# A new order table for attention with a causal conv gate: fewer masks on GpSimd, fewer unread products, and buffers named at another step

## The chip, the cores and the metric

The kernel runs on 1 core of one Trainium2 chip. The metric is the device time of one execution in microseconds (us), as a median of repeated runs. The engines are TensorE (PE; PEld is its weight load), VectorE (DVE), ScalarE (ACT), GpSimd (POOL) and SyncE (SP), which issues most of the transfers.

## What is computed

Eight batches, eight heads, 576 positions, head size 64. Each head is causal attention with a decay bias from cumulated gates s. The joined heads (512 wide) go through a causal convolution of five taps, a sigmoid, a product with a projection, and an output projection.

```python
def _attn_ref(q, k, v, s):                       # 8, 8, 576, 64
    scores = (1.0 / np.sqrt(D)) * np.matmul(q, k.transpose(0, 1, 3, 2))
    cum = np.cumsum(np.maximum(s, 0.0), axis=-1)
    bias = -(cum[:, :, :, None] - cum[:, :, None, :])
    scores = np.where(causal, -1000000000.0, scores + np.minimum(bias, 0.0))
    attn = softmax(scores)
    return np.matmul(attn, v)

def _moe_ref(x, w_val, conv_w, w_out):           # x: 8, 576, 512
    for k in range(5):
        gate_pre += conv_w[k][None, None, :] * xp[:, k:k + S, :]
    return (1.0 / (1.0 + np.exp(-gate_pre)) * (x @ w_val)) @ w_out
```

## The kernel before

The whole program is one straight line of named steps. A table, ORDER, lists them as `name.indices:engine:slots`. The engine letter is S (SP), T (PE), A (ACT), V (DVE) or G (POOL); the slots say which PSUM banks or which of several buffers the step writes. A loop at the end of `main_path` walks the table and calls the function of each step, so that each engine gets its instructions in the order of the table, and waits are set where one step needs another's data or buffer. There is no scheduler behind it.

The work falls into 32 units, numbered n: batch n // 4 and pair of heads n % 4. For each unit:

- `ld_q`, `ld_k`, `ld_t`, `ld_v` load q, k, their last 64 rows (the tails) and v. `c_q`, `c_k` cast to bf16. `qt`, `qq`, `tt` transpose on PE, and `qe`, `te` copy the result from PSUM into QKT. Batch 0 is loaded by pairs of heads, the other batches whole or in halves.
- `s0`, `s1`, `s2` are three groups of score products into two PSUM banks, `e0`, `e1`, `e2` the exponentials of 2 x 512 columns into a P buffer (L556). The causal triangle of the four diagonal blocks, which lie in group 0, is masked in one of two ways. Either POOL clears it after the exponential (`mk`, an affine_select on 128 x 1024, L579), or PE adds a large negative number before it by two more products into the same banks (`future`, L518). `s4`, `e4` do the last 64 keys.
- `vp` scales v by the decay (POOL, L474); `av0`, `av` are P times V, 60 products a unit (L594); `rec`, `nm` divide by the sums; `xt` transposes back, `xe` copies to xT.
- The five taps: `t1` on DVE starts gp; each of `t2`, `t3`, `t4` is either one DVE instruction (L670), or a product `p2`, `p3`, `p4` on POOL (L654) or ACT (L652) into a pr buffer and an add `t` on POOL (L673). All taps of a unit update the same gp buffer in the table's order.
- `th` is the tanh of the gate on ACT, `val` the projection (L703), `glu` the gate product on DVE (L712). `out` is the output projection (L723), `oe` copies it to an ot buffer (ACT or DVE), `st` stores it.

The last four units, 28 to 31, are cut into two parts (positions 0 to 383 and 384 to 575) with names of their own: `u0` to `u3` for scores, `f0` to `f3` for exponentials of 128 x 768 (L570), `ml` for the small mask. Their other steps carry the part as a second index.

`wu` is an unread product: 512 columns of the identity times the identity into a bank that nobody reads (L620). `chk0` and `chk` look whether all reciprocals and conv ratios are in a safe range (L734 to L746), `cnt`, `cntc` and `flag` reduce that to one number, and every engine reads it for the final branch (L754, L807); a general path behind it isn't taken here.

Of the kernel before, what the change touches and what calls it, by code (L numbers as in the profile page):

```python
# [16 lines left out]
B, H, S, D = 8, 8, 576, 64  # L17
# [180 lines left out]
centre:V s0.1:T:4+5:1 ld_k.1.0:S:2 s2.1:T:2+3 e0.1:A qt.0.2.q:T:1 c_k.0.2:V decT:T:0 ld_cw:S e2.0:A qt.0.2.k:T:4
mk.1:G wu.20:T:5 ld_k.1.1:S qe.0.2.k:V wu.21:T:5 wu.22:T:5 qe.0.2.q:A s1.1:T:6+7 c_k.0.3:V e2.1:A s0.2:T:4+5:2
c_q.0.3:G ld_v.0.2:S expw:A qt.0.3.q:T:1 e1.1:A s4.0.1:T:2+3 qe.0.3.q:V vp.0.0:G qt.0.3.k:T:0 qe.0.3.k:V e4.0.1:A  # L200
ld_q.1.0:S:3 e0.2:A s2.2:T:6+7 s1.2:T:2+3 vp.0.1:G av0.0:T:0+1 e2.2:A av.0:T ld_v.0.3:S mk.2:G rec.0:V av0.1:T:4+5
e1.2:A nm.0:V av.1:T c_k.1.0:G:2 s0.3:T:6+7:0 rec.1:V s2.3:T:2+3 e0.3:A nm.1:V ld_t.1:S cwT:T:0 xt.0:T:1 c_k.1.1:G
cwc:V xt.1:T:4 e2.3:A wu.23:T:6 xe.0:V ld_q.1.1:S vp.0.2:G qq.1.1:T:0:7 t1.0:V:0 s4.0.2:T:2+3 s1.3:T:5+6 e4.0.2:A
xe.1:V c_q.1.0:A:0 s4.0.3:T:2+3 mk.3:G t3.0:V ld_v.1.2:S e4.0.3:A t1.1:V:1 e1.3:A ld_v.1.1:S av0.2:T:2+3 vp.0.3:G
av.2:T t2.0:V ld_v.1.0:S qe.1.3:A tt.1:T:5 ld_v.1.3:S qe.1.2:V p4.1:G:0 p4.0:A:1 ld_v.1.4:S ld_wv:S:4 av0.3:T:6+7
av.3:T te.1:A rec.2:V ld_t.2:S t4.1:G c_q.1.1:G nm.2:V s0.6:T:0+1:1 rec.3:V xt.2:T:5 nm.3:V e0.6:A t4.0:G s0.7:T:2+3:2
xe.2:V s2.6:T:6+7 e0.7:A qq.1.0:T:0:1 t1.2:V:2 mk.6:G p2.1:A:0 s1.6:T:2+3 t3.2:V qe.1.0:A ld_q.2:S:0 mk.7:G qe.1.1:V
e2.6:A t3.1:V s1.4:T:0+1 e1.6:A s0.4:T:6+7:0 t2.2:V ld_k.2:S:1 xt.3:T:4 e0.4:A s0.5:T:2+3:0 t2.1:G t4.2:V s2.4:T:6+7
xe.3:V wu.24:T:5 e2.4:A vp.1.0:G mk.4:G wu.25:T:5 t1.3:V:3 wu.26:T:5 wu.27:T:5 ld_wo:S:2 wu.28:T:5 e1.4:A s4.1.3:T:6+7
ld_t.3:S t3.3:V wu.29:T:5 wu.30:T:5 e4.1.3:A s1.5:T:0+1 t4.3:V wu.31:T:5 th.2:A:0 ld_q.3:S:3 vp.1.2:G av0.4:T:6+7  # L210
th.1:A:1 av.4:T t2.3:V e0.5:A vp.1.1:G cast_wv:G rec.4:V av0.6:T:4+5 nm.4:V av.6:T e1.5:A s2.5:T:2+3 rec.6:V
s1.7:T:6+7 nm.6:V e2.5:A xt.4:T:0 ld_v.2.2:S c_q.2:G:1 tt.2:T:1 xe.4:V th.0:A:2 av0.5:T:2+3 t1.4:V:2 av.5:T te.2:A
ld_v.2.4:S val.3.0:T:4 th.3:A:3 p4.4:G:1 rec.5:V val.3.1:T:1 nm.5:V e1.7:A val.1.0:T:5 glu.3.0:V t4.4:G xt.5:T:2
c_k.2:A:2 glu.3.1:V ld_v.2.1:S val.1.1:T:3 glu.1.0:V s2.7:T:6+7 glu.1.1:V qq.2.0:T:1:5 vp.1.3:G xe.5:V val.0.0:T:3
t2.4:V e2.7:A val.0.1:T:4 t1.5:V:1 p2.5:G:0 qe.2.0:A av0.7:T:6+7 glu.0.0:V glu.0.1:V ld_v.2.3:S val.2.0:T:3 t2.5:G
p3.5:A:1 t3.4:V av.7:T ld_v.2.0:S qe.2.1:A qq.2.1:T:4:2 ld_k.5:S:4 rec.7:V cast_wo:G nm.7:V val.2.1:T:0 qe.2.3:A
xt.6:T:5 glu.2.0:V xt.7:T:1 xe.6:V qe.2.2:A s0.9:T:6+7:1 glu.2.1:V s1.9:T:2+3 p4.5:G:0 xe.7:V out.0.2:T:0 e0.9:A
t1.6:V:0 out.0.0:T:4 t3.5:G t1.7:V:3 e1.9:A ld_k.3:S:0 t4.6:V s1.8:T:6+7 oe.0.2:A:0 s0.8:T:2+3:0 mk.9:G oe.0.0:A:1
t3.7:V val.7.0:T:0 e0.8:A ld_t.4:S out.0.3:T:4 t2.6:V p3.6:G:1 e1.8:A t2.7:V out.0.1:T:2 t3.6:G th.4:A:4 t4.7:V
val.4.0:T:3 st.0.2:S val.7.1:T:7 glu.4.0:V th.7:A:3 val.4.1:T:1 t4.5:G oe.0.3:V:2 th.6:A:1 ld_v.3.2:S s2.8:T:5+6  # L220
glu.7.1:V s4.2.3:T:3+4 glu.7.0:V e2.8:A val.6.0:T:7 glu.4.1:V vp.2.0:G val.6.1:T:0 glu.6.0:V e4.2.3:A ld_v.3.3:S
oe.0.1:V:3 s0.10:T:5+6:2 th.5:A:2 c_q.3:G:0 s2.9:T:3+4 glu.6.1:V av0.8:T:1+2 e2.9:A av.8:T val.5.0:T:0 ld_q.5:S:1
e0.10:A rec.8:V nm.8:V vp.2.1:G s2.10:T:3+4 val.5.1:T:7 e2.10:A glu.5.0:V s1.10:T:1+2 glu.5.1:V s0.11:T:5+6:0 vp.2.2:G
# [616 lines left out]
```

## Time and profile before

| | us |
|---|---|
| three runs | 188.97, 189.09, 189.77; median 189.09 |
| profiled execution, first to last instruction | 187.6 |
| PE busy / DVE / ACT / POOL in it | 170.1 / 163.3 / 170.6 / 164.5 |
| first full exponential starts | 7.85 |
| last full exponential (unit 27) starts | 150.28 |
| last gate product starts | 181.77 |

The page gives no time of its own for the profiled execution beside its span; the median is 1.5 us above the span. The matmuls' ends are modelled, so PE's busy time is no measure of how full PE is. Transfers keep the 16 DMA engines near full until about 130 us and nearly idle afterwards, apart from the stores.

### The profile page before, as it was taken

Reading aid. Unit: us, or ns where it says so; the run is one execution under the profiler, and the core shown is the slowest. Engines: PE = TensorE matmul, PEld = TensorE weight load, DVE = VectorE, ACT = ScalarE, POOL = GpSimd, SP = SyncE. Lnnn points to the kernel's source line nnn. Section 1 sums busy time; section 2 is a strip of 40 time slices with the busy share of each in tenths; the row PEclk is TensorE's granted clock in tenths of the full one; section 3 lists DMA queues with packets and bytes.
Section 4 is the critical chain, followed back from the end, with each engine's and each line's share of the span. In section 5 each row is a group of like instructions: output and inputs, shape, how many; then the busy total and the mean of one; then the engine's idle time right before and its main releaser. Section 6 shows DMA issues by size and latency. Waiting matters only on the chain.

```text
span 187.6 us, 6637 instructions
## 1 busy us (share of the span) xinstructions
PE 170.1 (91%) x2704; PEld 113.5 (60%) x2720; DVE 163.3 (87%) x321; ACT 170.6 (91%) x230; POOL 164.5 (88%) x149
## 2 busy tenths in 40 slices
PE   6898885888899998998978999999999999999991
PEld 2556573476757765576745667586566865776560
DVE  4355999878997899999999899998989899999980
ACT  2589899899999999999999999999999999999772
POOL 5267999899999999999978999999999989899610
PEclk9999999999999999999999999999999999999999
DMA  5998999999999999999298999899541003401164
GB/s 164 274 277 246 231 225 243 343 388 341 193 232 304 277 303 258 389 270 283 71 248 184 274 333 325 193 314 247 164 162 66 3 0 115 171 3 56 61 224 175
DMA packets 62283, 40.46 MB, mean 216 GB/s; under 512 B 47333, under 2 KB 49381, under 8 KB 62250
## 3 DMA queue, kind: packets, MB, share of 16 engines
q1 hardware_dynamic: 61706, 39.49, 77.1%
q8 instruction: 22, 0.36, 0.8%
q10 hardware_dynamic: 544, 0.52, 0.8%
q14 instruction: 11, 0.09, 0.2%
HBM read 30.57 MB, written 9.44 MB: 213 GB/s over the span
## 4 chain that ended last, share of the span: by engine, by line
PE 50%; ACT 15%; SPq 9%; DMA 8%; issue 6%; POOL 5%; DVE 4%; ACTq 0%; POOLq 0%; DVEq 0%
PE bank L723 14%; PE bank L703 11%; PE bank L594 10%; ACT P L556 9%; PE bank L505 7%; DMA vst<-in_v_dram 6%; SPq L435 3%; PE bank L629 3%; PE bank L626 3%; POOL gp L673 2%; DMA first<-in_k_dram 2%; ACT th L690 2%; SPq L471 2%; ACT QKT L373 2%; SPq L467 2%
## 5 line engine op out<-in xcount | busy, mean ns | idle before, releaser
L556 ACT ACTIVATE P<-bank 128x1024 bf16<-128x1024 f32 x84 | 82.9, 1042 | 4.1 <-PE bank L505 3.0
L670 DVE SCALAR_TENSOR_TENSOR gp<-bank,cwr,gp 128x574 f32<-128x574 bf16 (+6 forms) x72 | 52.3, 740 | 0.9 <-POOL gp L673 0.5
L673 POOL TENSOR_TENSOR gp<-gp,pr 128x572 f32<-128x572 f32 (+6 forms) x36 | 45.1, 1259 | 4.4 <-DVE gp L670 1.7
L474 POOL TENSOR_TENSOR Vp<-vst,w 128x650 bf16<-128x650 f32 x32 | 40.7, 1288 | 2.8 <-DMA vst<-in_v_dram 1.8
L505 PE MATMUL bank<-QKT 64*128 64x128 bf16 (+4 forms) x592 | 37.2, 237 | 4.8 <-ACT P L556 1.8
L703 PE MATMUL bank<-xT,wv 128*128 128x288 bf16 (+2 forms) x256 | 38.5, 287 | 1.1 <-ACT P L556 0.5
L594 PE MATMUL bank<-Vp,P 128*128 128x65 bf16 x960 | 36.0, 194 | 2.4 <-POOL Vp L474 1.1
L594 PEld LDWEIGHTS <-P 128*128 128x128 bf16 x960 | 33.2, 97 | 6.8 <-issue 1.5
L723 PE MATMUL bank<-wo,glu 128*128 128x512 bf16 x128 | 34.1, 380 | 1.5 <-issue 0.5
L505 PEld LDWEIGHTS <-QKT 64*128 64x128 bf16 x592 | 19.4, 94 | 22.3 <-issue 14.6
L712 DVE SCALAR_TENSOR_TENSOR glu<-th,bank 128x288 bf16<-128x288 f32 (+2 forms) x64 | 27.5, 445 | 2.0 <-ACT th L690 0.9
L703 PEld LDWEIGHTS <-wv 128*128 128x128 bf16 x256 | 22.4, 97 | 11.0 <-issue 4.8
L654 POOL TENSOR_TENSOR pr<-xT,cwr 128x572 f32<-128x572 bf16 (+6 forms) x28 | 28.3, 1020 | 0.6 <-ACT xT L373 0.6
L373 ACT COPY QKT<-bank 128x1024 bf16<-128x1024 bf16 (+1 forms) x26 | 24.2, 966 | 3.8 <-PE bank L489 2.9
L613 DVE TENSOR_TENSOR xn<-bank,recs 128x640 bf16<-128x640 f32 (+2 forms) x36 | 26.8, 745 | 0.6
L665 DVE SCALAR_TENSOR_TENSOR gp<-xT,cwr,bank 128x576 f32<-128x576 bf16 (+2 forms) x36 | 26.4, 741 | 0.7
L579 POOL TENSOR_SCALAR_AFFINE_SELECT P<-P 128x1024 bf16<-128x1024 bf16 (+1 forms) x22 | 22.3, 1021 | 4.2 <-ACT P L556 4.2
L690 ACT ACTIVATE th<-gp,cwr 128x576 f32<-128x576 f32 x28 | 22.0, 794 | 0.1
L723 PEld LDWEIGHTS <-glu 128*128 128x128 bf16 x144 | 12.4, 98 | 13.2 <-issue 1.6
L373 ACT COPY ot<-bank 128x512 f32<-128x512 f32 x26 | 15.2, 610 | 1.5 <-PE bank L723 1.0
L626 PE MATMUL bank<-ident,xn 128*128 128x128 bf16 x164 | 14.9, 219 | 0.7 <-ACT P L556 0.3
L373 POOL CAST qkb<-qkf 128x2048 bf16<-128x2048 f32 (+1 forms) x9 | 14.4, 1619 | 0.0
(66 smaller groups left out, 174.8 us busy)
## 6 DMA issues: line engine op xcount, KB each, us to landing
out_dram<-ot SPq DMA_DIRECT2D x36, 256.0 KB, 4.3
vst<-in_v_dram SPq DMA_DIRECT2D x28, 256.0 KB, 5.9
first<-in_q_dram SPq DMA_DIRECT2D x6, 512.0 KB, 6.0
first<-in_k_dram SPq DMA_DIRECT2D x6, 512.0 KB, 6.2
qkf<-in_q_dram SPq DMA_DIRECT2D x6, 512.0 KB, 6.7
qkf<-in_k_dram SPq DMA_DIRECT2D x6, 512.0 KB, 7.3
vst<-in_v_dram SPq DMA_DIRECT2D x15, 128.0 KB, 5.4
first<-in_q_dram SPq DMA_DIRECT2D x4, 256.0 KB, 5.3
```

The costliest lines, as they stand in the source:

```text
L373: (act.copy if e is act else e.tensor_copy)(dst, src)
L474: e.tensor_tensor(Vps[b % 2][:, :, HP[p]], vslot(b)[:, :, HP[p]], w[:, :, b * 8 + 2 * p:b * 8 + 2 * p + 2].unsqueeze(3).to_broadcast([128, ...
L505: pe.matmul(ps[:, hh, c0:c0 + nq], QKTs[b % 2][r, 1, p, k0:k0 + 128], QKTs[b % 2][r, 0, p, q0:q0 + nq], **kw)
L556: act.activation(out=Pt(n)[:, :, step * 512:(step + 1) * 512], in_=pair((f"s{step}", n)), func=AF.Exp, scale=0.125)
L594: pe.matmul(ps[:, o:o + 65], lhsT, Vps[b % 2][:, kb, 2 * p + w, :], start=(kb == 0), stop=(kb == qb))
L613: vec.tensor_tensor(xns[b % 2][:, g, p * 128:(p + 1) * 128].rearrange("t g (w d) -> t w g d", w=2), ps[:, :, :, 0:64], recs[:, n, :, g].un ...
L654: pool.tensor_tensor(pr, xTs[b % 2][:, c, 4 + lo - m:4 + hi - m], r.to_broadcast([128, hi - lo]), ALU.mult)
L670: vec.scalar_tensor_tensor(gp[:, lo:hi], xps(n, *h)[:, lo - m:hi - m], r, gp[:, lo:hi], ALU.mult, ALU.add)
L673: pool.tensor_tensor(gp[:, lo:hi], gp[:, lo:hi], prs[at[f"p{m}", n, *h][0]][:, lo:hi], ALU.add)
L703: pe.matmul(ps, wv[:, dc, c * 128:(c + 1) * 128], xTs[b % 2][:, dc, 4 + lo:4 + hi], start=(dc == 0), stop=(dc == 3))
L712: vec.scalar_tensor_tensor(glu2[:, c, o + lo:o + hi], th[:, lo:hi], 1.0, ps, ALU.add, ALU.mult)
L723: pe.matmul(bank_of(u, i), glu2[:, c, i * 128:i * 128 + 128], wo[:, c, :], start=(c == 0), stop=(c == 3))
```

## The change

The table is replaced as a whole. Counted by kind:

| step | before | after |
|---|---|---|
| masks on POOL (`mk`, `ml`) | 18 and 4 | 4 and 0 (units 3, 11, 12, 22) |
| unread products | 32 | 12 |
| casts of q and k: ACT, DVE, POOL | 3, 4, 17 | 2, 2, 20 |
| tap products: ACT, POOL | 8, 28 | 4, 36 |
| tap adds `t2` to `t4`: DVE, POOL | 72, 36 | 68, 40 |
| QKT copies: ACT, DVE | 26, 10 | 23, 13 |
| output copies: ACT, DVE | 26, 10 | 28, 8 |
| xT copies: ACT, DVE | 12, 24 | 11, 25 |

The loads and stores keep their number. The units still come in nearly the same sequence; within a unit the score groups and exponentials may now come in any order, so the P buffer is named at the exponential (slot of `e0` to `e2`, `f0` to `f3`) and not at `s0`. The numbers of buffers (BUFS) are the same.

```diff
-ld_k.0.0:A ld_q.0.0:S ld_k.0.1:A wu.0:T:0 ld_t.0:S wu.1:T:7 wu.2:T:0 wu.3:T:7 ld_s:S wu.4:T:0 ld_q.0.1:S wu.5:T:7
+ld_k.0.1:A ld_t.0:S ld_k.0.0:A ld_q.0.0:S ld_q.0.1:S ld_k.0.2:S ld_k.0.3:S ld_s:S ld_v.0.0:S wu.0:T:7 wu.1:T:6
...
-    Pt = lambda n, h=None: Ps[at["s0" if h is None else f"u{2 * h}", n][1]]
+    split = lambda n: n in splits
+
+    def Pt(n, h=None):
+        steps = ("e0", "e1", "e2") if h is None else (f"f{2 * h}", f"f{2 * h + 1}")
+        return Ps[next(at[f, n] for f in steps if (f, n) in at)[0]]
...
-            split = ("u0", n) in at
-            g = ((3, 1)[h] if split else 4)
-            d = Pt(n, h if split else None)[:, :, 0:128 * g].rearrange("k w (g q) -> k w g q", g=g)
+            g = ((3, 1)[h] if split(n) else 4)
+            d = Pt(n, h if split(n) else None)[:, :, 0:128 * g].rearrange("k w (g q) -> k w g q", g=g)
...
-        two = at["val", n, 0][0]
-        j = two[hf] if isinstance(two, list) else at["val", n, hf][0]
+        j = at["val", n, hf][0]
...
+    splits = {int(name.split(".")[1]) for name, *_ in steps if name.startswith("u0.")}
```

The first place is SP, the start of the program. `first` is the tile that takes q and k of batch 0, `tail` the last 64 rows of all heads, `gp` holds s here, `vst` holds v. Before:

```order
L430 DMA first<-in_q_dram 128x2x256
L458 DMA tail_105<-in_q_dram 64x8x64
L458 DMA tail_105<-in_k_dram 64x8x64
L376 DMA gp_121<-in_s_dram 64x576
L430 DMA first<-in_q_dram 128x2x256 x2
L430 DMA first<-in_k_dram 128x2x256
L467 DMA vst_92<-in_v_dram 128x4x64 x2
L468 DMA vst_92<-in_v_dram 64x2x64
```

And after:

```order
L458 DMA tail_105<-in_q_dram 64x8x64
L458 DMA tail_105<-in_k_dram 64x8x64
L430 DMA first<-in_q_dram 128x2x256 x2
L430 DMA first<-in_k_dram 128x2x256 x2
L376 DMA gp_121<-in_s_dram 64x576
L467 DMA vst_92<-in_v_dram 128x4x64 x2
L468 DMA vst_92<-in_v_dram 64x2x64
```

The two tails moved ahead of the first q tile, and s moved behind four tiles of q and k. ACT's queue issues the first two k tiles in both.

The second place is POOL in the split units near the end. `gp` is the sum of taps, `pr` a tap product, `P` a buffer of exponentials; a pr row is a product, a gp row an add. Before:

```order
L673 TENSOR_TENSOR gp_119<-gp_119,pr_134 128x380
L579 AFFINE_SELECT P_118<-P_118 128x2x128
L654 TENSOR_TENSOR pr_134<-xT_114,cwr 128x381
L673 TENSOR_TENSOR gp_119<-gp_119,pr_135 128x382
L673 TENSOR_TENSOR gp_121<-gp_121,pr_134 128x381
L579 AFFINE_SELECT P_116<-P_116 128x2x128
L654 TENSOR_TENSOR pr_135<-xT_114,cwr 128x380
```

And after (L657 is the product and L676 the add in the new file):

```order
L657 TENSOR_TENSOR pr_135<-xT_114,cwr 128x381
L676 TENSOR_TENSOR gp_120<-gp_120,pr_135 128x381
L657 TENSOR_TENSOR pr_135<-xT_114,cwr 128x382
L676 TENSOR_TENSOR gp_120<-gp_120,pr_135 128x382
L676 TENSOR_TENSOR gp_122<-gp_122,pr_134 128x380
L657 TENSOR_TENSOR pr_135<-xT_114,cwr 128x192
L676 TENSOR_TENSOR gp_119<-gp_119,pr_135 128x192
```

The small masks are gone from there, and more of the taps are a product and an add on POOL.

The third place is the end of DVE. `glu` is the gate product, `stat` and `ok` are the check, `ot` is an output tile. Before:

```order
L712 SCALAR_TENSOR_TENSOR glu_115<-th_126,bank 128x192
L712 SCALAR_TENSOR_TENSOR glu_115<-th_124,bank 128x192
L734 TENSOR_REDUCE stat<-recs 128x1
L735 TENSOR_REDUCE stat<-recs 128x1
L745 TENSOR_SCALAR ok<-stat 128x2
L746 TENSOR_SCALAR ok<-stat 128x2
L758 TENSOR_REDUCE okcnt<-bank 1x1
```

And after, down to the end of `chk0`; the same five rows from L734 to L758 follow it:

```order
L712 SCALAR_TENSOR_TENSOR glu_115<-th_126,bank 128x192
L712 SCALAR_TENSOR_TENSOR glu_115<-th_125,bank 128x192
L373 COPY ot_132<-bank 128x512
L739 TENSOR_TENSOR okt<-cwr 128x20
L740 TENSOR_SCALAR ok<-okt 128x20
L734 TENSOR_REDUCE stat<-recs 128x1
L735 TENSOR_REDUCE stat<-recs 128x1
```

`chk0` (L739, L740 and the first L734 and L735) stood among the work of unit 27. It stands now behind `oe.3.8`, DVE's last output copy; the very last copy, `oe.3.7`, is ACT's in both.

More of the change, by code (lines that the diff above doesn't have):

```diff
@@ L198 @@
[L198 to L222, printed above, removed]
@@ L294 @@
+glu.28.1:V out.3.4:T:6 t2.31.1:G glu.29.1:V glu.30.1:V th.31.1:A:2 outa.3.8:T:3 oe.3.4:A:0 glu.31.1:V out.3.8:T
+st.3.4:S outa.3.7:T:2 oe.3.8:V:4 out.3.7:T chk0:V st.3.8:S oe.3.7:A:1 st.3.7:S chk:V cnt:T:4 cntc:V flag:S
 """
@@ L674, in tap @@
         return f
-    split = lambda n: ("u0", n) in at
     def thof(n):
```

175 lines of the change are left out of this document (99 added, 76 removed).

## Prediction

> **What bounds the kernel now.** I read the page first, for the busy shares and the slices, then the table of stretches, then the groups by shape, the waits, and the timeline of the first 35 us and of the last 35. From the page, busy time by engine and two rows of slices (4.7 us each):
>
> ```profile
> PE 170.1 (91%) x2704; PEld 113.5 (60%) x2720; DVE 163.3 (87%) x321; ACT 170.6 (91%) x230; POOL 164.5 (88%) x149
> ...
> ACT  2589899899999999999999999999999999999772
> POOL 5267999899999999999978999999999989899610
> ```
>
> No engine has a stage to itself: all are near 90%, and the scalar engine (ACT) and GpSimd (POOL) are low only at the two ends. The table of stretches (start and end, length, then busy us and instructions of PE, weight load, DVE, ACT, POOL) parts start, middle and tail:
>
> ```profile
> 0.00:10.20 10.20, 8.23 (x52) 3.83 (x52) 4.70 (x15) 4.80 (x7) 4.52 (x14) 1.00 0.89 221
> 10.20:152.50 142.30, 131.14 (x2298) 90.41 (x2310) 129.29 (x229) 137.12 (x174) 135.74 (x107) 1.00 0.90 242
> 152.50:187.60 35.10, 30.72 (x362) 19.24 (x362) 29.30 (x78) 28.71 (x51) 24.22 (x29) 1.00 0.30 108
> ```
>
> In the middle ACT idles 5.2 us of 142.3, POOL 6.6, DVE 13.0. So the middle lasts as long as ACT's work, with POOL close behind; PE's 131.1 holds the drains of short chains and unread products. In the tail POOL idles 10.9 us of 35.1.
>
> ```profile
> ACT P L556 <- PE bank L505: 3.0, 7, 0.7
> ```
>
> This row of the waits says how seldom ACT waits for scores: 7 times in its 84 full exponentials, 3.0 us in all.
>
> **The change part by part.** The sum is made against the profiled 187.6 us; the three runs have a median of 189.09, so 1.5 us are added at the end. What the moved steps cost, from the groups by shape (busy us, mean ns of one, then idle before):
>
> ```profile
> L556 ACT ACTIVATE P<-bank 128x1024 bf16<-128x1024 f32 x84 | 82.9, 1042 | 4.1 <-PE bank L505 3.0 <-issue 0.4 <-PE bank L594 0.3
> L373 ACT CAST qkb<-first 128x2048 bf16<-128x2048 f32 x1 | 1.9, 1898 | 0.0
> L652 ACT ACTIVATE pr<-bank,cwr 128x572 f32<-128x572 bf16 x4 | 3.2, 789 | 0.0
> L373 ACT COPY QKT<-bank 128x1024 bf16<-128x1024 bf16 x22 | 21.8, 1034 | 0.7 <-PE bank L629 0.6
> L373 ACT COPY ot<-bank 128x512 f32<-128x512 f32 x26 | 15.2, 610 | 1.5 <-PE bank L723 1.0 <-ACT ot L373 0.6
> L579 POOL TENSOR_SCALAR_AFFINE_SELECT P<-P 128x1024 bf16<-128x1024 bf16 x18 | 20.6, 1153 | 4.2 <-ACT P L556 4.2
> L654 POOL TENSOR_TENSOR pr<-xT,cwr 128x572 f32<-128x572 bf16 x9 | 10.3, 1147 | 0.2 <-ACT xT L373 0.2
> L673 POOL TENSOR_TENSOR gp<-gp,pr 128x572 f32<-128x572 f32 x13 | 18.3, 1406 | 1.7 <-DVE gp L670 1.3
> ```
>
> *ACT up to its last full exponential (unit 27).* The new order has one whole-batch cast less (1.9 us), two tap products less (5 to 3: 1.6), three QKT copies less (two of 1.03, one of half that size: 2.6), and three output copies more (3 x 0.61 = 1.8). One score group and one xT copy change sides of this point and cancel. That is 4.3 us less. Neighbours overlap: 84 x 1.042 = 87.5 us of exponentials took 82.9, a factor of 0.95. Term: **-4.1 us**.
>
> *POOL up to the same point.* Fourteen masks leave (14 x 1.15 = 16.1), three casts come (one whole of about 1.9, two small, 3.1 together), two products (2.3) and one add (1.4). That is 9.3 us less on an engine that idled 6.6 in the middle, so POOL stops being a second bound there. How much of ACT's 5.2 us of idle goes with it no row tells. The ends are 0 and -5.2; I take a little under half, as its waits name PE and not POOL, while PE waits in turn for POOL's products and masks. Term: **-2.4 us**. DVE sheds about 2 us there, off the path.
>
> *Masks on PE.* Each full mask becomes two products that run side by side:
>
> ```profile
> L518 PE MATMUL bank<-fut,fut 64*128 64x512 bf16 x20 | 3.8, 376 | 0.0
> L620 PE MATMUL bank<-ident 128*128 128x512 bf16 x32 | 10.7, 451 | 1.4 <-POOL ident masks.py:199 1.4
> ```
>
> 28 more of them at 3.8/20 = 0.19 us are 5.3 us, the four small masks under 1 us, and 20 fewer unread products give 20 x 0.33 = 6.7 back. Cost: nothing, covered by PE's idle and by scores standing ready for ACT (the 7 waits above). If that cover is gone, each masked unit delays its first exponential by 0.2 us: 14 x 0.2 = 2.8 us. The stores and loads keep their number on SP; another order of them costs nothing while V tiles come in time, and about 1 us either way if not.
>
> *The start.* SP's queue begins with both tails of batch 0, and q of pair 0 is its third transfer instead of its first. From the timeline (start, us, engine, line, and what ended the idle time before):
>
> ```profile
> 1.33 0.73 SPq L458 DMA_DIRECT2D tail<-in_q_dram  x1
> 1.44 3.60 PE L620 MATMUL bank<-ident 128*128 128x512 bf16 x8 [1.44 <-POOL ident masks.py:199]
> 4.95 0.76 DVE L373 CAST qkb<-first 128x512 bf16<-128x512 f32 x2 [1.54 <-DMA first<-in_k_dram]
> 7.85 1.02 ACT L556 ACTIVATE P<-bank 128x1024 bf16<-128x1024 f32 x1 [0.49 <-PE bank L505]
> 8.26 0.45 DVE L379 TENSOR_SCALAR gp<-gp 64x576 f32<-64x576 f32 x1 [2.54 <-DMA gp<-in_s_dram]
> 33.53 1.25 PE L620 MATMUL bank<-ident 128*128 128x512 bf16 x5
> ```
>
> At 4.95 the first k and q tiles were in, 256 KB each by their shape; at 8.26 the s tile, and with it 1,168 KB: 656 KB in 3.31 us, 198 KB/us. Now q of pair 0 ends the first 1,024 KB (two k, two tails of 128, one q), so I estimate it at 4.95 + 512/198 = 7.5. From the cast at 4.95 to the exponential at 7.85 went 2.9 us, so the first full one comes at about 10.4. What ACT has done by then, from the groups:
>
> ```profile
> L373 ACT ACT_TABLE_LOAD x1 | 1.3, 1283 | 1.9 <-issue 1.9
> L373 ACT CAST QKT<-bank 128x512 bf16<-128x512 f32 x6 | 3.6, 606 | 0.4 <-PE bank L480 0.4
> L532 ACT ACTIVATE P<-bank 128x128 bf16<-128x128 f32 x4 | 1.2, 298 | 0.3 <-PE bank L518 0.3
> ```
>
> The table load, a tail copy, a QKT copy of like size and one small exponential are 2.8 us, against 4.80 before in 10.2 us. Term: **+2.0 us** (0 if the later stalls of the first 30 us shrink as much; +3.5 with the rival of the clock below).
>
> *The tail, to the last gate product (glu).* From the timeline and the groups:
>
> ```profile
> 150.28 1.04 ACT L556 ACTIVATE P<-bank 128x1024 bf16<-128x1024 f32 x1
> 151.09 1.41 POOL L673 TENSOR_TENSOR gp<-gp,pr 128x572 f32<-128x572 f32 x1 [0.62 <-DVE gp L670]
> 178.97 0.59 POOL L673 TENSOR_TENSOR gp<-gp,pr 128x192 f32<-128x192 f32 x1 [0.46 <-DVE gp L670]
> 181.77 0.35 DVE L712 SCALAR_TENSOR_TENSOR glu<-th,bank 128x192 bf16<-128x192 f32 x1 [0.40 <-PE bank L703]
> L654 POOL TENSOR_TENSOR pr<-xT,cwr 128x380 f32<-128x380 bf16 x3 | 2.4, 824 | 0.0
> L654 POOL TENSOR_TENSOR pr<-xT,cwr 128x192 f32<-128x192 bf16 x3 | 1.5, 512 | 0.4 <-ACT xT L373 0.4
> L673 POOL TENSOR_TENSOR gp<-gp,pr 128x380 f32<-128x380 f32 x3 | 2.9, 997 | 0.0
> L579 POOL TENSOR_SCALAR_AFFINE_SELECT P<-P 128x256 bf16<-128x256 bf16 x4 | 1.7, 426 | 0.0
> ```
>
> Last full exponential to last glu was 182.1 - 150.3 = 31.8 us. In it POOL worked from 151.1 to 179.6, 28.5 us with gaps of 0.5 and 0.6 among them; I put its work at 26.6 and its idle at 1.9. The new order gives it there two more full products (2.3), one more of 0.82 and three of 0.51 in the half units (2.4), three more adds there (one of 1.0, two of 0.59: 2.2), and takes the four small masks (1.7) away: 31.7 us. Its very last add now stands ahead of the last tanh and glu (0.9 us with their hand-overs), and it starts 0.6 us after the exponential: 0.6 + 31.7 + 0.9 = 33.2, if it never waits. Term: **+1.5 us**, with ends 0 (it came in ahead) and +5 (it waits as an engine that alternates with DVE may). DVE's work there falls by 1.1, ACT's by 1.6: neither binds.
>
> *The end.* The check of the reciprocals (chk0) moves behind the last copy on DVE. The old run:
>
> ```profile
> 156.15 0.38 DVE L739 TENSOR_TENSOR okt<-cwr 128x20 f32<-128x20 f32 x1
> 157.01 0.43 DVE L735 TENSOR_REDUCE stat<-recs 128x1 f32<-128x280 f32 x1
> 182.65 0.59 ACT L373 COPY ot<-bank 128x512 f32<-128x512 f32 x1 [0.58 <-ACT ot L373]
> 183.58 0.17 DVE L758 TENSOR_REDUCE okcnt<-bank 1x1 int32<-1x24 f32 x1 [1.04 <-PE bank L749]
> L807 SPq EVENT_SEMAPHORE  x8: 17/17/17, 185.5 to 186.2; - x8
> L373 DVE COPY ot<-bank 128x512 f32<-128x512 f32 x10 | 6.8, 683 | 0.0
> ```
>
> The flag was ready at 183.75, 1.6 us after the last glu. Now DVE copies from 0.5 to 1.2 us after it, the moved check takes 157.44 - 156.15 = 1.3, the old check 0.5, product and last reduction 0.5: 3.5 us after, 1.9 later. SP's eight waits behind the branch came 1.8 us behind the flag, and the run ends 1.4 us after them; the last store hides part. Ends 0.6 and 1.9; I take **+1.3 us**, nearer to the end in which it all shows, since every engine reads the flag before it can stop. The faster path of the last copy (DVE beside ACT) saves nothing once the flag is last.
>
> *Sum:* -4.1 - 2.4 + 2.0 + 1.5 + 1.3 = -1.7; 187.6 - 1.7 + 1.5 = **187.4 us**. Half a per cent of the median, 0.95 us, is what a measurement here can tell from no change: faster is below 188.1, slower above 190.0.
>
> **The rivals.** *POOL gets ahead (faster).* With 9.3 us less before the last full exponential it is not late at the tail, and the tail term is 0; ACT's idle of the first 30 us shrinks so that the start costs 0.5: -4.1 - 2.4 + 0.5 + 0 + 1.3 = -4.7, 184.4 us. For it: POOL's idle in the slices is at the ends only. Against: every tap needs a transpose of its own unit, which comes late.
>
> *POOL binds the tail (slower).* Place: from the last full exponential to the last tap. Each add on POOL stands between two taps of DVE on the same gp buffer, so the two wait for each other in turn. It has 18 adds to make; a wait of 0.5 us, as before the adds at 151.09 and 178.97, ahead of eight of them is 4 us of idle: tail +5.5, sum +2.3, 191.4 us. It decides from 3.2 us of tail term on, that is 1.7 us of idle in POOL's last 33. For it: the row at 178.97 waits so already. Against: DVE has 1.1 us less to do there.
>
> *The clock of PE (no change).* Eight products took 3.60 us at the start, five took 1.25 at 33.5: 0.42 against 0.22 from start to start. PE has five unread products at first instead of eight, then waits for the tails, so the half rate lasts into the scores. At 0.2 us for each of ten score steps that is +2.0: sum +0.3, 189.4 us. The Trainium skill (TensorE: Matmul & The Clock Gate, Part 1: The HAM clock gate) says that the array starts at half rate and is released by about 3.4 us of sustained activity; by that rule five products do not release it, and this rival would be the case. The spacing of the first eight agrees, while the page's PEclk row does not show it. Against it: ACT, not PE, is full once scores flow.
>
> **How the numbers follow.** Forecast 0.40 (own range 186 to 189.3: faster 0.25, same 0.13, slower 0.02); POOL ahead 0.20 (all faster); POOL in the tail 0.24 (slower 0.22, same 0.02); clock 0.16 (same 0.08, slower 0.08). Faster 0.45, same 0.23, slower 0.32. The range, 183.9 to 191.9, leaves out a third of the faster rival and four tenths of the slower one, and a little of the rest.
>
> **What would show it.** Right: the first full exponential at 10 to 10.5 us; ACT idle under 3.5 us between it and the last; that last one at about 146; last glu 33 us behind it; flag some 3.5 us behind glu and SP's waits later than the last store. Wrong: a first exponential before 9 us, PE at 427 ns beyond 12 us, POOL idle for over 2 us after the last full exponential, or waits on V tiles that were not there.

## The result: slower, 198.7 us against 189.3

The new order took 198.71 us (median of four runs, 198.06 to 199.25), the kernel before 189.33 in the same comparison: a ratio of 1.050, 95% interval 1.046 to 1.054. The profiled execution spans 196.2 us against 187.6.

From the page of the new kernel, the busy time of the engines and three rows of slices (4.9 us each):

```profile
PE 171.6 (87%) x2719; PEld 114.1 (58%) x2736; DVE 168.5 (86%) x317; ACT 165.7 (84%) x223; POOL 161.3 (82%) x146
...
ACT  2279799897999989999899899949999799984851
POOL 5235998959999999967999699599879789999950
PEclk9999999699999999999999999999999999999999
```

ACT is busy for 4.9 us less than before and POOL for 3.2 us less (the prediction's terms for middle and tail came to 5.9 and 4.2), and both idle more. The table of stretches, parted at the starts of the first and the last full exponential (11.25 and 155.36), first of the new kernel (start and end, length, busy us and instructions of PE, weight load, DVE, ACT, POOL, then clock, DMA share, GB/s):

```profile
0.00:11.25 11.25, 7.08 (x38) 3.77 (x39) 4.28 (x15) 2.74 (x5) 5.05 (x16) 1.00 0.89 237
11.25:155.36 144.11, 130.00 (x2243) 88.37 (x2256) 130.00 (x221) 133.59 (x170) 125.08 (x95) 0.99 0.85 234
155.36:196.20 40.84, 34.49 (x441) 21.95 (x443) 34.19 (x81) 29.34 (x51) 31.18 (x35) 1.00 0.27 99
```

And the same two later stretches of the kernel before:

```profile
7.85:150.28 142.43, 131.17 (x2278) 89.83 (x2291) 128.87 (x228) 137.25 (x174) 135.41 (x106) 1.00 0.92 247
150.28:187.60 37.32, 32.94 (x401) 21.12 (x402) 31.52 (x81) 30.93 (x55) 25.82 (x31) 1.00 0.28 101
```

So 3.4 us were lost at the start, 1.7 in the middle and 3.5 from the last full exponential on. In the middle ACT shed 3.7 us of busy time and POOL 10.3, and the stretch still became longer: ACT's idle in it went from 5.2 to 10.5 us, POOL's from 7.0 to 19.0. From the timeline, the steps named in the prediction (the third of the three exponentials that start at 153.53 is the last full one):

```profile
11.25 1.94 ACT L560 ACTIVATE P<-bank 128x1024 bf16<-128x1024 f32 x2 [0.57 <-PE bank L505]
...
132.44 0.77 ACT L691 ACTIVATE th<-gp,cwr 128x576 f32<-128x576 f32 x1 [2.52 <-POOL gp L676]
...
153.53 2.85 ACT L560 ACTIVATE P<-bank 128x1024 bf16<-128x1024 f32 x3 [1.09 <-PE bank L505]
...
189.86 0.35 DVE L712 SCALAR_TENSOR_TENSOR glu<-th,bank 128x192 bf16<-128x192 f32 x1 [0.17 <-ACT th L685]
...
193.05 0.17 DVE L758 TENSOR_REDUCE okcnt<-bank 1x1 int32<-1x24 f32 x1 [0.26 <-PE bank L749]
```

| step | forecast | new profile |
|---|---|---|
| first full exponential starts | 10.4 | 11.25 |
| from there to the last one | 142.4 - 6.5 = 135.9 | 144.1 |
| last full exponential to the end of the last glu | 33.2 | 34.9 |
| end of the last glu to the end of the run | 5.5 + 1.3 = 6.8 | 6.0 |

### The profile page after: what moved, and what is told of

Same layout as the page of the kernel before. It is cut to its first block, busy times and chain, and to the rows that moved or that the text cites. A ratio compares the mean times of both kernels' runs of the same rounds, so it can differ in the third digit from the quotient of the medians.

```text
span 196.2 us, 6664 instructions
## 1 busy us (share of the span) xinstructions
PE 171.6 (87%) x2719; PEld 114.1 (58%) x2736; DVE 168.5 (86%) x317; ACT 165.7 (84%) x223; POOL 161.3 (82%) x146
## 4 chain that ended last, share of the span: by engine, by line
PE 27%; ACT 23%; DVE 19%; POOL 16%; issue 7%; DMA 4%; SPq 1%; ACTq 0%; DVEq 0%; POOLq 0%
ACT P L560 14%; POOL gp L676 8%; PE bank L597 7%; POOL pr L657 5%; PE bank L723 5%; PE bank L505 5%; DMA tail<-in_k_dram 4%; PE bank L703 4%; DVE glu L712 4%; DVE xn L616 4%; DVE gp L673 4%; ACT QKT L373 3%; DVE QKT L373 2%; DVE gp L668 2%; ACT th L691 2%
## 5 line engine op out<-in xcount | busy, mean ns | idle before, releaser
L673 DVE SCALAR_TENSOR_TENSOR gp<-bank,cwr,gp 128x574 f32<-128x574 bf16 (+5 forms) x68 | 51.5, 760 | 2.0
L676 POOL TENSOR_TENSOR gp<-gp,pr 128x573 f32<-128x573 f32 (+6 forms) x40 | 48.7, 1220 | 4.7 <-ACT pr L655 1.8
L505 PE MATMUL bank<-QKT 64*128 64x128 bf16 (+4 forms) x592 | 39.7, 240 | 8.9 <-ACT P L560 4.6
L657 POOL TENSOR_TENSOR pr<-xT,cwr 128x574 f32<-128x574 bf16 (+6 forms) x36 | 35.2, 984 | 6.2 <-DVE xT L373 4.8
L703 PE MATMUL bank<-xT,wv 128*128 128x288 bf16 (+2 forms) x256 | 36.8, 286 | 0.4 <-DVE xn L616 0.3
L505 PEld LDWEIGHTS <-QKT 64*128 64x128 bf16 x592 | 20.1, 95 | 25.9 <-issue 19.0
L712 DVE SCALAR_TENSOR_TENSOR glu<-th,bank 128x288 bf16<-128x288 f32 (+2 forms) x64 | 26.1, 447 | 3.3 <-ACT th L691 2.0
L373 ACT COPY QKT<-bank 128x1024 bf16<-128x1024 bf16 (+1 forms) x23 | 21.7, 984 | 1.6 <-PE bank L489 1.1
L373 POOL CAST qkb<-first 128x2048 bf16<-128x2048 f32 (+1 forms) x11 | 14.3, 1313 | 7.8 <-DMA first<-in_q_dram 4.9
L373 ACT COPY ot<-bank 128x512 f32<-128x512 f32 x28 | 16.4, 608 | 2.0 <-issue 1.3
L373 DVE COPY QKT<-bank 128x1024 bf16<-128x1024 bf16 (+1 forms) x13 | 13.2, 1012 | 5.1 <-PE bank L489 5.1
```

Of the source, the lines that this page charges most:

```text
L373: (act.copy if e is act else e.tensor_copy)(dst, src)
L505: pe.matmul(ps[:, hh, c0:c0 + nq], QKTs[b % 2][r, 1, p, k0:k0 + 128], QKTs[b % 2][r, 0, p, q0:q0 + nq], **kw)
L657: pool.tensor_tensor(pr, xTs[b % 2][:, c, 4 + lo - m:4 + hi - m], r.to_broadcast([128, hi - lo]), ALU.mult)
L673: vec.scalar_tensor_tensor(gp[:, lo:hi], xps(n, *h)[:, lo - m:hi - m], r, gp[:, lo:hi], ALU.mult, ALU.add)
L676: pool.tensor_tensor(gp[:, lo:hi], gp[:, lo:hi], prs[at[f"p{m}", n, *h][0]][:, lo:hi], ALU.add)
L703: pe.matmul(ps, wv[:, dc, c * 128:(c + 1) * 128], xTs[b % 2][:, dc, 4 + lo:4 + hi], start=(dc == 0), stop=(dc == 3))
```

## The experiments

All ratios are to the kernel before on the same chip, with 95% intervals; 0.01 is 1.9 us. The kernel before took 188.5 to 189.4 us in these comparisons, so kernels are compared with each other by their ratios. A "join" takes the first steps of one table and then the other table's remaining steps in its own order; a few banks and buffers are renamed where the two meet, and tap products, masks and unread products that only the part not taken needs are left out.

**Is the middle set by ACT, or by any one engine?** Four kernels with the old table each leave about 4 us of work out of one engine.

```diff
# e13_act
+NO_COPY = {(2, 1), (0, 5), (1, 1), (1, 0), (1, 5), (1, 8), (1, 7)}
     def out_evac(e, u, i):
-        copy(e, ots[at["oe", u, i][0]], bank_of(u, i))
+        if (u, i) not in NO_COPY:
+            copy(e, ots[at["oe", u, i][0]], bank_of(u, i))
# e14_dve: steps taken out
-t2.10:V  t4.11:V  t3.14:V  t4.16:V  t2.19:V
# e15_pool: steps taken out
-t3.8:G  t4.14:G  t4.19:G
# e16_pe
+HALF = {(0, 6), (0, 8), (0, 4), (0, 5), (1, 1), (1, 2), (1, 0), (1, 3), (1, 4), (1, 6)}
-            for c in (range(4) if ("outa", u, i) not in at else ...
+            for c in (range(2) if (u, i) in HALF else range(4) if ("outa", u, i) not in at else ...
```

> The table before, with seven output copies on ACT between 80 and 134 us left out (7 x 0.61 = 4.3 us of its work; those tiles are stored without their result). By the prediction's first step (the middle lasts as long as ACT's work, factor 0.95) 4.1 us faster, 185.0 us. If another engine sets the middle, under 1.5 us faster.

> The table before, with five taps on DVE between 72 and 123 us left out (5 x 0.805 = 4.0 us of its work; five taps are missing from the result). By the prediction DVE's work there lies off the path: within 0.5 us of before. If DVE sets the middle, 3 to 4 us faster.

> The table before, with three adds on POOL at 72, 95 and 124 us left out (3 x 1.41 = 4.2 us of its work; three taps are missing from the result). By the prediction's second step (9.3 us less on POOL gives 2.4 us) 1.1 us faster. If POOL sets the middle, 3 to 4 us faster; if it is off the path, within 0.5 us.

> The table before, with two of the four products left out in ten output tiles between 65 and 140 us (20 products of 512 columns at 0.22 us from start to start: 4.3 us of PE's work; those tiles lack half their sum). By the prediction PE's work there is covered: within 0.5 us of before. If PE's queue sets the middle, as the 1.8 us of the run with the masks on PE suggest (28 products at 0.19 us), 1.5 to 4 us faster.

| left out | ratio | interval |
|---|---|---|
| 4.3 us of ACT | 0.9995 | 0.9956 to 1.0035 |
| 4.0 us of DVE | 1.0028 | 0.9990 to 1.0067 |
| 4.2 us of POOL | 0.9989 | 0.9956 to 1.0023 |
| 4.3 us of PE | 0.9985 | 0.9946 to 1.0024 |

None gained: at most 1 us of 4 fits into any interval, and zero fits into all. Each left out what it was meant to: 7 instructions of ACT, 5 of DVE, 3 of POOL, 20 of PE. The amounts in the table are sums of durations; busy time, in which overlaps count once, fell by 3.2 to 4.4 us. The first line of each page shows it in its own column: ACT 3.2 us less than before in e13,

```profile
PE 170.6 (91%) x2704; PEld 114.1 (61%) x2720; DVE 163.0 (87%) x321; ACT 167.4 (89%) x223; POOL 164.1 (88%) x149
```

DVE 3.3 less in e14,

```profile
PE 171.5 (91%) x2704; PEld 114.1 (61%) x2720; DVE 160.0 (85%) x316; ACT 170.7 (91%) x230; POOL 163.7 (87%) x149
```

POOL 4.0 less in e15,

```profile
PE 170.6 (91%) x2704; PEld 114.2 (61%) x2720; DVE 163.9 (87%) x321; ACT 170.1 (91%) x230; POOL 160.5 (85%) x146
```

and PE 4.4 less in e16:

```profile
PE 165.7 (89%) x2684; PEld 111.8 (60%) x2700; DVE 163.3 (88%) x321; ACT 170.1 (91%) x230; POOL 164.3 (88%) x149
```

With ACT relieved, its waits for scores rose from 3.0 us in 7 times to:

```profile
ACT P L557 <- PE bank L506: 4.8, 11, 1.0
```

The work went and waiting took its place. That four nearly full engines in a fixed order are late for each other in turn is how I read it; the runs show only that none of the four sets the stretch alone. Two rivals are left untested. Two engines could set it together: no run relieves two at once, as the new table was to do with ACT and POOL. And the transfers could: from the first full exponential to 130 us the 16 DMA engines were full in the kernel before (share 1.02, the last column but one),

```profile
7.85:130.00 122.15, 111.48 (x1946) 76.53 (x1957) 109.86 (x193) 117.00 (x148) 115.51 (x90) 1.00 1.02 271
```

and 0.99 to 1.03 in the four kernels here, which all move the same bytes. Against the transfers: the waits that end with one make 9.2 us in the kernel before, and 6.2 of these lie in its first 9 us.

**What do the masks cost on PE?** The old table without the 18 `mk` and `ml` steps that the new one takes from POOL.

```diff
-mk.0:G mk.1:G mk.2:G mk.4:G mk.6:G mk.7:G mk.9:G mk.13:G mk.14:G mk.18:G mk.19:G mk.20:G mk.24:G mk.27:G
-ml.28:G ml.29:G ml.30:G ml.31:G
```

> The table before, with the same 18 masks taken from POOL that the new table takes (14 full, 4 small) and made by PE, all else as it was. If a mask on PE lies in the way of the exponentials at 0.2 us each, 2.8 us slower than before. If PE's cover holds, no slower, and up to 2.4 us faster, since POOL loses 17.8 us of work and ACT idles 5.6 us between the first and the last full exponential.

191.08 us, ratio 1.0115 (1.0074 to 1.0157): 2.2 us slower, with 17 us less work on POOL. Its middle stretch in the table of stretches:

```profile
7.50:151.90 144.40, 135.41 (x2316) 90.69 (x2316) 128.40 (x228) 137.24 (x174) 120.25 (x92) 0.99 0.88 244
```

And the row of its waits that says what POOL did with the time (1.7 us in 3 times before):

```profile
POOL gp L673 <- DVE gp L670: 11.3, 8, 3.8
```

The middle is 2.0 us longer, the tail (37.4) as long as before. POOL waits for taps of DVE instead of masking. ACT's waits for PE at a full exponential went from the 3.0 us in 7 times of the prediction's row to 3.9 in 9, for the mask products (L518) and the scores (L505):

```profile
ACT P L556 <- PE bank L518: 2.3, 5, 0.9
ACT P L556 <- PE bank L505: 1.6, 4, 0.9
```

That is about 1 of the 2 us; where the other one goes is open. The reverse, on the new table:

```diff
 e0.13:A:1
+mk.13:G
 ... and so for the other 13 units
```

> The new table with the 14 full masks back on POOL, each directly behind the exponential of its unit, and so 28 products of 64x512 less on PE, all else as it was. If masks on PE cost the new order what they cost the old one (1.8 us), 196.9 us. If POOL, with 16 us of work more, holds the taps up instead, 200 us or more: then the move of the masks was needed for the new share of taps.

209.69 us, ratio 1.110 (1.102 to 1.118), 11 us slower than the new table as it is. So with the masks back in these places the new share of taps is far too much; the move paid for the taps and not for time. Not all of the 11 us need be POOL's work: in this run's profile PE's clock was at half for 17 us, against 3.4 in the new kernel's (last section).

**The start.** A join: the old table up to step 146 (23.5 us), then the new.

```diff
-ORDER = new
+ORDER = old[:146] + [step for step in new if step not in old[:146]]
```

> The first 146 steps are those of the table before (23.5 us of its profile, up to the scores of units 6 and 7), the rest those of the new table in its own order. If the new start's 3.4 us (first full exponential at 11.25 against 7.85) are carried to the end, this takes 198.7 - 3.4 = 195.3 us. If they are made up for later anyway (the lag of the exponentials was down to 1.1 us at the 24th), it takes 197.6 or more, and the start is not a cause.

197.77 us, ratio 1.0446 (1.0378 to 1.0514), about 1.1 us better than the new table; the intervals overlap. Its profile had the exponentials 0.7 to 1.6 us ahead of the new kernel's from unit 4 to unit 22, and 0.2 behind from unit 24 on, after a stretch of half clock at 133.9 us that the new kernel's profile doesn't have. The 3.4 us at the first exponential are thus worth 1 to 1.5, by an estimate that these runs alone don't secure.

**Loads and stores on SP.** SP stands still for 8 us twice in the first 130 us of the new kernel, each time in front of a store whose tile isn't copied yet. (Besides the eight stores the edit gives one output copy, `oe.0.5`, another ot buffer.)

```diff
 st.0.2 ... st.0.1
+st.0.0 st.0.3
 ...
-st.0.6
 ld_k.5 ld_t.6 ld_v.4.4 ld_q.4 ... ld_v.4.0
+st.0.6 st.0.4 st.0.5
 ... (in the same way st.1.4 behind ld_v.6.1, st.1.7 and st.1.6 behind ld_v.7.4)
```

> The new table with eight stores moved on SP's queue, nothing else: two whose tiles had long been copied go up, six that waited for their copies go behind the loads that stood after them. If SP's idle of 8 us at 65.0 and 8.1 us at 106.8 (each in front of a store that waits for its copy) makes the loads late and with them Vp on POOL and the gates, the lag of 2 to 3 us that builds up between the 60th and the 72nd exponential goes: 196.2 us or less. If the loads had time, it stays within 0.7 us of 198.7.

204.88 us, ratio 1.083 (1.077 to 1.090): 6 us slower than the new table. Up to 90 us the exponentials came within 0.2 us of where they were, so those loads had not been late; then an output copy waited for the store that should free its tile and now stood behind loads. The row of its waits:

```profile
ACT ot L373 <- DMA out_dram<-ot: 8.4, 3, 5.6
```

The idea fell, and the price of the opposite mistake was seen. It does not say what the second of the two places costs by itself.

**V tiles.** From the waits of the new kernel:

```profile
POOL Vp L474 <- PE bank L703: 2.5, 1, 2.5
```

The row names PE, but the instruction waits for several semaphores, and the last two of them belong to transfers of v. They came at 124.7 us, 9.7 after the last reader of that buffer on POOL had ended (115.0). Behind the scaling came the taps of unit 19, and the tanh at 132.44 shown above.

```diff
-vp.6.1:G ... vp.6.3:G ... p4.19:G p3.19:G t4.19:G t3.19:G
+p4.19:G p3.19:G t4.19:G t3.19:G vp.6.1:G vp.6.3:G
```

> The new table with two steps moved on POOL and nothing else: the scaling of v for units 25 and 27 (vp.6.1, vp.6.3) goes behind the taps of unit 19 instead of ahead of them. In the new kernel's profile POOL waited 2.5 us ahead of it for tiles of v that came 9.9 us after their buffer was free, and the tanh of unit 19 at 132.4 waited 2.5 us for POOL with the exponentials behind it. If this is a cause, 198.7 - 2.5 = 196.2 us or less (5 us less of POOL work stands ahead of that tanh); if other work is late there too, 198 or more.

196.35 us (195.88 to 198.79), ratio 1.0471 (1.0396 to 1.0547). From its timeline, POOL with the scalings behind the adds:

```profile
123.09 2.24 POOL L657 TENSOR_TENSOR pr<-xT,cwr 128x572 f32<-128x572 bf16 x2 [1.58 <-DVE xT L373]
125.29 2.88 POOL L676 TENSOR_TENSOR gp<-gp,pr 128x572 f32<-128x572 f32 x2
128.12 5.01 POOL L474 TENSOR_TENSOR Vp<-vst,w 128x650 bf16<-128x650 f32 x4
```

And ACT with the tanh of unit 19, which now waits for nothing:

```profile
128.69 0.88 ACT L691 ACTIVATE th<-gp,cwr 128x576 f32<-128x576 f32 x1
```

The tanh comes 3.7 us earlier and the flag 2.2 us; 0.9 of these were there from unit 5 on, for another reason (the clock, below). So 1.3 us are this wait's, in a profile of one execution each. By ratio the kernel is only 0.6 us better than the new table, and the intervals overlap. Start and v together:

> Two changes of earlier runs together on the new table: the first 146 steps of the old table (1 us faster by itself, with 1.5 us less lag up to unit 20), and the two scalings of v on POOL behind the taps of unit 19 (2.3 us faster by itself). If the two are separate causes, 198.7 - 1.0 to 1.5 - 2.3 = 195 us; if one hides the other, 196.3.

195.40 us, ratio 1.0369 (1.0295 to 1.0443): 2.5 us better than the new table, and here the intervals don't overlap. So start and v cost something together. That is nearer to two separate causes (195) than to one hidden by the other (196.3), but the interval, 1.4 us either way, holds both.

**Unread products.**

```diff
 wu.4:T:7
+wu.12:T:0 wu.13:T:1 wu.14:T:2 wu.15:T:3
 tt.0:T:0
 ... (16 more, ahead of qq.1.1, s4.0.2, av.2, s4.1.3, s0.4, s1.7, s0.6, xt.4 and four ahead of s1.22)
```

> The new table with 20 unread products more, as many as before had: 4 ahead of the first tail transposes, 3 at 24 to 26.5 us, 9 at 32 to 40 us, 4 at 132.5 to 134 us, each where PE idled. The granted clock of PE was half for 3.4 us from 35.6 in the new kernel and at full speed all through in the one before; a run whose steps were the same up to there had one such stretch more and was 1.2 us later behind it. If fewer unread products cost by that, no stretch is left and the time falls to 197.5 or less; if the clock doesn't matter, it stays or rises by up to 1 us.

198.43 us, ratio 1.0523 (1.0476 to 1.0571), no different from the new table. The stretch at 35.6 us with PE's clock at half (the 6 in the row PEclk above) was gone in its profile, another one lay at 8.4, and the products put ahead of `s1.22` delayed unit 22. The profile is of the slowest of its four executions (200.23 us, mean clock 0.986). The other three had a mean clock of 0.996 to 1, against 0.988 to 0.991 in the four of the new kernel, and a median of 198.0 us where the kernel before took 188.5, against 198.7 on 189.3. So the unread products do keep the clock up in most executions, and nothing is gained by it.

**The tail.** Joins both ways around the last full exponential, and one at 122 us.

```diff
# e6_newtail
+ORDER = old[:900] + [step for step in new if step not in old[:900]]
# e2_tail
+ORDER = new[:910] + [step for step in old if step not in new[:910]]
# e5_body
+ORDER = old[:740] + [step for step in new if step not in old[:740]]
```

> The first 900 steps are those of the table before (up to the scores behind its last full exponential), the rest those of the new table: the new tail alone, with two products and two adds more on POOL for the half units and the moved check. If the new tail binds by itself (37.8 us from the last full exponential of unit 27 to the flag, against 33.5), 189.3 + 4.3 = 193.6 us. If its length came from gates that the middle had left behind, 189.3 + 0.5 for the check's place = 190, up to 191.

> The first 910 steps are those of the new table (up to its last full exponential, of unit 27), the rest those of the table before, with its engines: less work for POOL in the half units, and the check of ratios ahead of the last work. If POOL binds the new tail, the 3.9 us by which the last gate product came later behind the last full exponential (35.7 against 31.8) and 0.5 us of the end go: 198.7 - 4.4 = 194.3 us. If the tail is only late because the gates of units 24 to 27 come late out of the middle, it stays above 197.

> The first 740 steps are those of the table before (its first 122 us, up to scores of unit 21 and 22), the rest those of the new table. In the profile of the first run with the old start the exponentials kept pace with before up to unit 15 and fell behind by 3.8 us from unit 15 to unit 22. If that loss comes of the new order in that stretch itself, it is gone here and the time is 199 - 2 - 3.8 = 193.2 us. If it comes of what the new order leaves for later (gates, copies), it is as late as the last run, over 196.

The new tail behind the old body: 193.72 us, ratio 1.028 (1.0225 to 1.0335), 5.3 us slower than the kernel before. Up to the last full exponential (150.4) it runs as the old kernel does; from there it needs 41.9 us instead of 37.3. So the new tail behind the old body costs 4.6 us of the span:

```profile
150.40:192.30 41.90, 34.61 (x441) 22.16 (x446) 34.54 (x83) 29.40 (x50) 31.11 (x35) 1.00 0.25 90
```

The old tail behind the new body, e2, did not give this back: 199.39 us, ratio 1.0495, no better than the new table. From its last full exponential (157.24) it needs 40.3 us, against 40.8 in the new kernel and 37.3 in the old one:

```profile
157.24:197.50 40.26, 33.97 (x438) 21.76 (x435) 33.96 (x82) 31.77 (x56) 24.36 (x29) 1.00 0.28 100
```

By what was expected of it, the new kernel's tail is late because of gates that come late out of the middle; by e6 the new tail is late by itself. (The 35.7 us in that expectation count from the exponential before the last; from the last it is 34.9.) So the two costs don't simply add. e2 is no clean run either: PE's clock was at half in two stretches where the new kernel had one (last section), and its late gates are in an order that the old tail wasn't made for. In e5 (199.02, 1.0585) the join itself made a copy wait for its tile, 4.4 us in one piece, on ACT, so it settles nothing.

What in the tail? The check by itself, then POOL's work, then the last unit's places.

```diff
# e9_chk, on the old table
-... chk0:V ...                glu.31.1:V chk:V
+...                           glu.31.1:V chk0:V chk:V
# e10_less_pool, on e6
-p2.29.0 t2.29.0  p3.28.0 t3.28.0  p3.29.0 t3.29.0  p4.30.0 t4.30.0   (all :G)
# e17_last, on e6; e18_last_less, the same on e10
+DVE: rec.31.1 nm.31.1 behind glu.28.0; xe.31.1 t1.31.1 behind t1.30.1
+PE:  xt.31.1 behind out.3.1 (ahead of out.3.0, out.3.6, out.3.5)
```

> The table before with one step moved, the check of the ratios (chk0), from among the work of unit 27 to directly behind the last gate product on DVE. By the term of the prediction the flag comes 1.3 us later (the moved check takes 1.3 us ahead of the old one) and all of it shows: 190.4 us on 189.1. If the run's end is set by the last store, or the profile's net 0.5 us of the new kernel is the rule, 189.1 to 189.6.

> As the run with the old body and the new tail (193.7 us), but four tap products and their four adds on POOL are left out (p and t 2.29.0, 3.28.0, 3.29.0, 4.30.0): 7.3 us less work for POOL between 169 and 177 us, none added elsewhere; four taps of the half units are missing from the result. If POOL, which never waits in that tail from 159 to 185 us, binds it, the time falls by 3 to 5 us, to 189 to 190.7. If the order of the other engines binds, it stays above 192.5.

> Old body and new tail (193.7 us), with the last unit's steps moved forward: rec and nm of 31.1 on DVE behind the gate product of 28.0 (from 181.5 to about 177.3 us), its transpose on PE ahead of out.3.0, its copy and first tap on DVE behind the first tap of 30.1. If POOL alone closes the tail, no gain (193.2 to 194.2). If the place of the last unit's steps in the two queues is what binds, 1.2 to 2 us less: 192 us.

> The same moves on top of the run with four products and four adds less on POOL (192.8 us; the same four taps missing from the result). If POOL and the two queues bind the tail side by side, only both together show: 190.5 to 191.3 us. If neither is the cause, 192.3 or more.

| kernel | us | ratio | interval |
|---|---|---|---|
| e9, check moved alone | 188.85 | 0.998 | 0.994 to 1.002 |
| e6, new tail | 193.72 | 1.028 | 1.0225 to 1.0335 |
| e10, with 7.1 us less on POOL | 192.82 | 1.021 | 1.015 to 1.027 |
| e17, last unit forward | 194.73 | 1.025 | 1.019 to 1.030 |
| e18, both | 193.51 | 1.023 | 1.019 to 1.027 |

The moved check costs nothing that this run can tell. The rest gave back little or nothing: POOL's busy time in the tail is down to 24.0 us in e10, less than the 25.8 of the old kernel, and the tail still takes 41.5 us; by what was expected of e18, neither POOL's work nor the last unit's places is the cause. The timeline of e10 shows where POOL stands instead:

```profile
167.53 2.06 POOL L678 TENSOR_TENSOR gp<-gp,pr 128x380 f32<-128x380 f32 x2
176.16 0.51 POOL L659 TENSOR_TENSOR pr<-xT,cwr 128x192 f32<-128x192 bf16 x1 [6.57 <-ACT xT L375]
177.34 0.59 POOL L678 TENSOR_TENSOR gp<-gp,pr 128x192 f32<-128x192 f32 x1 [0.67 <-DVE gp L675]
...
183.28 0.59 POOL L678 TENSOR_TENSOR gp<-gp,pr 128x192 f32<-128x192 f32 x1 [0.24 <-DVE gp L675]
```

POOL, done with the first halves at 169.6, waits 6.6 us for an xT of a second half; then come six products and six adds, one row, to 183.9, and the run ends behind them. The chain of e10 shows what the xT waited for, PE:

```profile
171.92 3.09 PE bank L705 x20
...
175.56 0.17 PE bank L631 x3
...
177.79 3.53 PE bank L725 x16
181.32 0.18 PE bank L631 x3
```

(L705 is the projection, L631 the transposes xt, L725 the output product there.) In the old tail the four second halves' transposes stood at 171.8, 175.0, 175.8 and 178.3 in PE's queue; in e6 at 177.6, 176.5, 178.6 and 182.3, behind projections and output products, though the tile for the first (`nm.28.1`) was ready at 170.6. And four of the old tail's last adds were POOL's, six in the new one. That these two make the 4.6 us is read from the chain of e10 and not shown: in e18 the last of the four transposes stood at 179.7 instead of 181.2 and nothing was gained, and its chain runs through DVE from 168 to 178 us before it reaches that row on POOL. DVE is a rival that no run tests: up to the last glu it was busy for 30.9 of the old tail's 31.8 us, and for 32.3 of 35.8 in e6. A kernel with the transposes of 28.1 to 30.1 moved forward, with fewer pairs in that last row, or with less work on DVE in the tail was not run.

No version in these runs beats the kernel before by more than the noise.

## Why the prediction was wrong

- *"So the middle lasts as long as ACT's work, with POOL close behind": the step that failed.* The counts of work were near (ACT 3.7 us less where 4.1 was charged after the factor, POOL 10.3 where 9.3 was counted); what work is worth was not. Terms of -6.5 us stood for it, and the stretch grew by 1.7. By e13 4.3 us of ACT are worth 0.1 us, by e15 4.2 us of POOL 0.2, neither different from nothing. What does set the stretch stays open (two engines together and the transfers were not tried). The row of 7 waits and 3.0 us was read as "scores stand ready"; it says only that ACT was seldom late in that one order. The Trainium skill (Perfetto Trace Analysis, Identifying the Most-Contended Engine) advises optimizing the engine with the highest occupancy first (and judging PE by other measures); with PE, ACT, DVE and POOL at 91, 91, 87 and 88% the traces do not agree, since relief of any one bought nothing.
- *Masks on PE, "cost: nothing":* 2.2 us by e4 (1.4 to 3.0). The price named for the case that the cover is gone, 2.8, lies in this interval, but its mechanism accounts for about half: ACT waited 0.9 us more for PE at its full exponentials. It is not PE's amount of work either, since 4.3 us less of it bought nothing in e16; that PE had no slack just where the masks fell is how I read it.
- *Order of loads, "costs nothing while V tiles come in time, and about 1 us either way if not":* they did not come in time. It cost 1.3 us by the profiles and 0.6 by ratio, so the size fits; the condition had not been checked.
- *The start, +2.0:* q was in at 7.15 (estimated 7.5), but from there to the exponential it took 4.1 us and not 2.9. The rival of the clock had the place: PE idled from 3.8 to 6.5, and behind that its products of 512 columns still came 0.43 us apart. (The clock of 1.00 in the first row of the stretches says nothing of this: the trace holds no clock record ahead of 11.69 us, and none ahead of 6.44 in the kernel before.) But more stood in the way than the clock. The first q was cast on POOL in 0.61 us instead of on DVE in 0.43, and the scores of the first full exponential came behind two other groups of the unit, s4 and s2. How the 1.2 us divide was not separated. The start was worth 1 to 1.5 us at the end.
- *The tail, +1.5:* 3.0 us to the last glu in the new kernel, 4.6 us of span in e6, the check included. POOL's work was rightly counted (31.7 against 31.2) and the sum then assumed "if it never waits"; it idled 3.7 us, one of the prediction's own signs of being wrong, as the waits on V tiles were. The rival "POOL binds the tail" named the stretch and the sign; its mechanism, waits scattered ahead of eight adds, was not the one seen. The order of PE's queue in the tail was not looked at, and that DVE, busy for 97% of the old tail up to the last glu, doesn't bind was said without a run.
- *The end, +1.3:* nothing by e9 (-0.3 us, within 0.8). The flag did come 3.0 us behind glu, near the 3.5 expected, but the rest of the run behind it shrank from 3.8 to 3.0 us.

Start 1.1, masks 2.2, v 1.3 and tail 4.6 make 9.2 us of the 9.4 lost. That they agree is partly luck: they were measured in different surroundings, start and v are clear of the noise only together, e2 gained nothing with the old tail, the masks and the tail share four small masks, and the half clock may hide among them. So the agreement is not a proof of the parts.

## What to carry to other kernels

When several engines are near 90% and the order is fixed by hand, a term "so much less work on engine X" is worth nothing until a run that simply leaves that work out has shown it. Added work and late places did cost time here, but not by their busy time either: 28 mask products and eight small ones, about 6 us by the prediction's count, cost 2.2, and a check of 1.3 us moved to the end cost nothing. So look at what stands ahead of the last-needed steps in each queue, and not only at the sums of busy time. And when a stretch is judged by one engine's few waits, ask what that engine would wait for next if it were faster.

## What was not expected of the hardware

PE's granted clock fell to half for stretches of 3.41 us in the middle of a run, in 16 of the 20 profiles here. The profile of the kernel before had none, the new one's one, and e12's one three times as long in one piece besides one of twice the length. The row of the new kernel for its stretch, the clock in the third column from the end:

```profile
35.60:39.00 3.40, 3.02 (x44) 2.30 (x45) 2.56 (x4) 3.08 (x4) 3.28 (x3) 0.50 1.12 345
```

The row PEclk of e3, with three of them:

```profile
PEclk9999999799999999999699999969999999999998
```

And of e12:

```profile
PEclk9997599757999999999999999999999999999998
```

It is not a property of the order alone: e9, which is the old kernel up to 156 us, had one at 32.2 us and still ended 0.5 us earlier than the old kernel's profile, and e7, the new kernel up to 122 us, had none and was 0.9 us earlier than the new one from unit 5 on. Nor did the new order bring it. The other executions of the kernel before have a mean clock each: in 62 of 72 it was 0.991 or less, which one such stretch alone makes (half of 3.41 in 188 us). So it is the usual case in both kernels. Half of these 62 took 188.9 us or more; of the ten others eight, at 1.0, took 187.5 to 188.1 and two, at 0.997, 189.7 and 190.2. What a stretch costs is thus not settled, but about 1 us would fit.

Over the 3.4 us ahead of a stretch PE was busy 39 to 59% in all but two cases, with no gap over 1.9 us. Cut into pieces of 3.413 us from each trace's first clock record on, the 20 profiles have 1,043 pieces at full clock, without those at the very end. All 14 in which PE was under 49% busy were followed by half clock, none of the 1,006 from 60% up, and 9 of the 23 between. The Trainium skill (TensorE: Matmul & The Clock Gate, Part 1: The HAM clock gate) states a free-running window of 3,413 ns and the half rate after an idle one. The length agrees to the nanosecond; that a window must be idle does not, half-full ones are enough here. The free-running window would also account for one order meeting it in one run and not in the next, which these runs show but do not prove.
